# Renumbering the FFN units of a fused HGRN2 and FFN kernel, and pacing its weight loads by landings

## Chip, cores and metric

One core of one Trainium2 chip. The metric is the device time of one execution in microseconds; a kernel is run three to six times beside the kernel before on the same chip. Some executions fall in a slower state; medians below are over all runs.

## The reference

```python
f = 1 / (1 + exp(-f_logit))                       # (4, 8, 768, 48) each of q, k, v, f_logit
for t in range(768):
    state = f[t][:, None] * state + outer(k[t], v[t])
    y[t]  = q[t] @ state
x = y.transpose(0, 2, 1, 3).reshape(3072, 384)
h = maximum(x @ w_in, 0)                          # w_in (384, 2048)
out = (h * h) @ w_out                             # w_out (2048, 384)
```

The kernel cuts the sequence into 24 chunks of 128 tokens. The 2,048 FFN units may stand in any order, as long as the columns of w_in and the rows of w_out are renumbered alike.

## The kernel before

A small planner simulates the engines with fixed durations and settles the order of instructions on each. The kernel is then emitted in that order, and the framework puts in the semaphore waits. The weights come in eight pieces, cast by DMAs that GpSimd issues; the loads of f, k, q and v, 192 KB each in 192-byte runs, come through SyncE's queue.

```python
LOADS = [0, 1, 2, "i0", 3, "i1", "i2", "i3", "o0", "o1", 4, "o2", "o3"] + list(range(5, NCH))
...
w_in = const.tile([C, KS, d_ff], BF16)            # 128 x 3 x 2048
w_out = const.tile([C, FS, d_model], BF16)        # 128 x 16 x 384
wi_view = moe_w_in.rearrange("(ks p) f -> p ks f", p=C)
wo_view = moe_w_out.rearrange("(fs p) f -> p fs f", p=C)

def load_w(kind, s, behind):                      # piece s of w_in or w_out, set off by v of a chunk
    def fn():
        if kind == "i":
            nc.gpsimd.dma_start(w_in[:, :, s * FW:(s + 1) * FW], wi_view[:, :, s * FW:(s + 1) * FW])
        else:
            nc.gpsimd.dma_start(w_out[:, s * FQ:(s + 1) * FQ, :], wo_view[:, s * FQ:(s + 1) * FQ, :])
    plan.add(f"cw{kind}{s}", "POOL", 1.0, fn, after=[f"vc.{behind}"], rank=-1, data=(2.4, 0))
...                                               # attention: cut
for x in range(m):                                # first FFN product, hp
    for ks in range(KS):
        nc.tensor.matmul(hp[:, x, :], w_in[:, ks, (f + x) * C:(f + x + 1) * C], xT[:, ks, lo:lo + W], ...)
...                                               # relu and square, then the second product, op
nc.tensor.matmul(st["o", i], hT[:, fs, tt * C:(tt + 1) * C], w_out[:, fs, :], ...)
```

GpSimd also casts v (vz) and computes the state update (sz), which needs tm from VectorE, which needs ds from TensorE. Every engine runs its own instructions in order.

## Time and profile before

| | before |
|---|---|
| median, lowest, highest of 3 runs | 192.5, 192.18, 196.64 us |
| span of the profiled run | 192.4 us |
| useful TensorE work, all | 161.6 us |
| useful TensorE work by 50 us, by 60 us | 23.7, 33.7 us |

"Useful" is the sum over matmuls of columns / 2.4 + 2.5 ns, idle fillers left out; the prediction explains it. The sums come out only if each matmul counts for at least 26 ns. The narrow ones, of 1 and 48 columns, do follow one another at 25 to 26 ns in the trace; without this floor the figures are 159.1, 23.1 us. The profiled run itself took 194.19 us. In timelines the columns are start, duration, engine, line, operation, and in brackets the idle time just before and what ended it. The lines that carry the reading are in the prediction.

### The profile page before, as it was taken

What the parts mean: (1) busy time and instruction counts of PE and PEld (TensorE: products, weight loads), DVE (VectorE), ACT (ScalarE), POOL (GpSimd) and SP (SyncE); (2) the same over time, 40 slices, a digit from 0 to 9 for tenths busy, and PEclk for the clock granted to TensorE, in tenths of its full rate; (3) what the DMA queues carried; (4) which work ended last, traced back from release to release, by engine and by line L of the source; (5) the groups of instructions that cost most, each with busy time, mean ns of one, the idle gap of its engine ahead of it and who ended that gap; (6) DMA issues with size and microseconds to landing.
All of it is one profiled execution on the core that took longest, in us unless ns stands there. A gap on an engine that the chain in (4) does not pass through costs nothing.

```text
span 192.4 us, 4720 instructions
## 1 busy us (share of the span) xinstructions
PE 177.5 (92%) x1810; PEld 119.9 (62%) x1810; DVE 126.6 (66%) x262; ACT 129.4 (67%) x275; POOL 45.0 (23%) x87
## 2 busy tenths in 40 slices
PE   6783999938999999999999999999999999999992
PEld 5562788924777867666666666666566566656561
DVE  5683647742688998997996787889668724244200
ACT  4451278811577968999999887988777766376410
POOL 5251941010403423504231331232231100000000
PEclk9998599985999999999999999999999999999999
DMA  6999999999999999198999899996989896311112
GB/s 120 191 151 199 172 193 184 187 165 197 188 160 200 163 174 197 24 193 167 177 180 173 157 201 191 169 187 128 186 157 171 266 303 233 97 41 41 46 43 79
DMA packets 123255, 31.05 MB, mean 161 GB/s; under 512 B 116576, under 2 KB 123232, under 8 KB 123232
## 3 DMA queue, kind: packets, MB, share of 16 engines
q1 hardware_dynamic: 119520, 27.60, 78.4%
q0 software_dynamic: 3712, 3.15, 10.4%
q8 instruction: 14, 0.23, 0.5%
q14 instruction: 9, 0.07, 0.1%
HBM read 25.17 MB, written 4.72 MB: 155 GB/s over the span
## 4 chain that ended last, share of the span: by engine, by line
PE 70%; DMA 10%; SPq 10%; ACT 3%; DVE 2%; issue 2%
PE op L491 33%; PE hp L446 25%; DMA io_q<-in_q_dram 10%; SPq L217 10%; PE at L344 3%; PE yp L367 3%; PE pc L288 1%; PE tr L320 1%; PE ds L407 1%; PE xp L381 1%; ACT hr L453 1%; ACT ob L501 1%; DVE hr L455 1%; PE pc L291 1%; ACT hT L460 0%
## 5 line engine op out<-in xcount | busy, mean ns | idle before, releaser
L446 PE MATMUL hp<-xT,w_in 128*128 128x384 bf16 (+2 forms) x528 | 79.9, 285 | 0.3 <-DVE xT L386 0.2
L491 PE MATMUL op<-w_out,hT 128*128 128x384 bf16 x384 | 79.6, 332 | 0.6 <-ACT ob L501 0.6
L453 ACT ACTIVATE hr<-hp 128x384 bf16<-128x384 f32 (+1 forms) x102 | 52.0, 512 | 24.5 <-PE hp L446 21.6
L446 PEld LDWEIGHTS <-w_in 128*128 128x128 bf16 x528 | 42.4, 99 | 18.0 <-issue 0.8
L462 DVE TENSOR_TENSOR hT<-hr 128x384 bf16<-128x384 bf16 (+1 forms) x87 | 33.4, 385 | 30.4 <-ACT hr L453 28.9
L491 PEld LDWEIGHTS <-hT 128*128 128x128 bf16 x384 | 36.0, 99 | 23.8 <-issue 2.9
L424 POOL TENSOR_TENSOR sz<-tm,en 48x192 bf16<-48x192 f32 x40 | 22.2, 555 | 68.8 <-DVE tm L415 26.5
L351 DVE TENSOR_TENSOR am<-at,ut 128x512 bf16<-128x512 f32 x48 | 31.6, 683 | 2.7 <-PE at L344 2.5
L282 POOL CAST vz<-io_v 128x384 bf16<-128x384 f32 x24 | 13.8, 583 | 38.1 <-DMA io_v<-in_v_dram 37.5
L501 ACT COPY ob<-op 128x384 f32<-128x384 f32 x21 | 10.0, 476 | 17.2 <-PE op L491 17.1
L460 ACT ACTIVATE hT<-hr 128x384 bf16<-128x384 bf16 (+1 forms) x33 | 17.8, 540 | 1.7 <-DVE hr L455 0.8
L277 ACT ACTIVATE e<-io_f 128x384 f32<-128x384 f32 x24 | 12.5, 522 | 9.1 <-DMA io_f<-in_f_logit_dram 9.1
L308 DVE TENSOR_TENSOR az<-io_k,ep 128x384 bf16<-128x384 f32 x24 | 14.3, 594 | 3.5 <-ACT ep L298 3.3
L312 DVE TENSOR_TENSOR az<-io_q,en 128x384 bf16<-128x384 f32 x24 | 15.2, 631 | 1.5 <-DMA io_q<-in_q_dram 1.4
L298 ACT ACTIVATE ep<-pc 128x384 f32<-128x384 f32 x24 | 11.7, 488 | 5.0 <-PE pc L291 2.4
L415 DVE TENSOR_TENSOR tm<-ds,sz 128x384 f32<-128x384 f32 x16 | 8.8, 550 | 8.4 <-PE ds L407 7.9
L278 ACT ACTIVATE pz<-e 128x384 bf16<-128x384 f32 x24 | 12.6, 523 | 0.8
L304 ACT ACTIVATE en<-pc 128x388 f32<-128x388 f32 (+1 forms) x24 | 11.8, 492 | 0.0
L522 PE MATMUL idle<-zero 128*128 128x128 bf16 x108 | 10.7, 247 | 1.0 <-DVE zero L247 1.0
L455 DVE TENSOR_SCALAR hr<-hp 128x384 bf16<-128x384 f32 (+1 forms) x18 | 10.3, 574 | 1.7 <-PE hp L446 1.7
L344 PE MATMUL at<-ts 64*128 64x128 bf16 x192 | 10.0, 226 | 0.8 <-DVE ts L328 0.8
L320 PE MATMUL tr<-ident,az 128*128 128x128 bf16 x88 | 7.7, 224 | 3.0 <-DVE az L312 2.4
(40 smaller groups left out, 135.2 us busy)
## 6 DMA issues: line engine op xcount, KB each, us to landing
io_f<-in_f_logit_dram SPq DMA_DIRECT2D x24, 192.0 KB, 4.2
io_k<-in_k_dram SPq DMA_DIRECT2D x24, 192.0 KB, 4.3
io_q<-in_q_dram SPq DMA_DIRECT2D x24, 192.0 KB, 4.3
io_v<-in_v_dram SPq DMA_DIRECT2D x24, 192.0 KB, 4.2
out_dram<-ob SPq DMA_DIRECT2D x24, 192.0 KB, 2.6
w_in<-in_moe_w_in_dram POOLq DMA_DIRECT2D x4, 384.0 KB, 7.7
w_out<-in_moe_w_out_dram POOLq DMA_DIRECT2D x4, 384.0 KB, 14.7
ts<-az SPq DMA_TRANSPOSE x13, 3.5
```

The costliest lines, as they stand in the source:

```text
L217: nc.sync.dma_start(t, srcs[n][b].rearrange("h s d -> s h d")[c * C:(c + 1) * C])
L282: nc.gpsimd.tensor_copy(vz[i % 4], st["v", i])
L308: nc.vector.tensor_mul(az[i % 4][:, H:, :D], st["k", i], st["ep", i])
L312: nc.vector.tensor_mul(az[i % 4][:, :H, :D], st["q", i], st["en", i][:, :HD].rearrange("p (h d) -> p h d", d=D))
L344: nc.tensor.matmul(ps[x][:, pr, :], ts[r, NP + pr, :], ts[r, pr, :], skip_group_check=True)
L351: nc.vector.tensor_mul(t, st["at", i][x], ut4)
L424: nc.gpsimd.tensor_mul(nx[r, :, D * x:D * (x + 1)], st["tm", i][r, :, D * x:D * (x + 1)], st["en", i][r, HD:HD + NP].unsqueeze(2).to_broad ...
L446: nc.tensor.matmul(hp[:, x, :], w_in[:, ks, (f + x) * C:(f + x + 1) * C], xT[:, ks, lo:lo + W], start=(ks == 0), stop=(ks == KS - 1), skip ...
L453: nc.scalar.activation(hr[:, :m, :], st["hp", c0, f][:, :m, :], AFT.Relu)
L460: nc.scalar.activation(st["hT", g][:, f:f + m, lo:lo + W], hr[:, :m, :], AFT.Square)
L462: nc.vector.tensor_mul(st["hT", g][:, f:f + m, lo:lo + W], hr[:, :m, :], hr[:, :m, :])
L491: nc.tensor.matmul(st["o", i], hT[:, fs, tt * C:(tt + 1) * C], w_out[:, fs, :], start=(fs == 0), stop=(fs == FS - 1))
```

## The change

The intent is twofold. With four consecutive w_out rows in one partition, a DMA writes runs of 3,072 bytes instead of 768. And each weight piece is now set off when a named load has landed (a one-element copy, `touch`, makes GpSimd wait for it), so that pieces and loads share the DMA engines more evenly; the planner models the two rings for this, and puts the casts of v ahead of the pieces (`rank=-2`).

```diff
+    SHARE = {"POOL": 0.7, "SP": 0.3}             # planner: how two busy rings share (rest of it cut)
-    LOADS = [0, 1, 2, "i0", 3, "i1", "i2", "i3", "o0", "o1", 4, "o2", "o3"] + list(range(5, NCH))
+    PACE = [4, 8, 10, 13, 13, 17, 18, 18]        # piece n goes behind this many loads
-    wo_view = moe_w_out.rearrange("(fs p) f -> p fs f", p=C)
+    wo_view = moe_w_out.rearrange("(s p x) f -> p s x f", p=C, x=FQ)
+            if pace and x != "v":
+                nc.gpsimd.tensor_copy(touch[:1, :1], st[x, c][:1, 0, :1])
-                nc.gpsimd.dma_start(w_out[:, s * FQ:(s + 1) * FQ, :], wo_view[:, s * FQ:(s + 1) * FQ, :])
+                nc.gpsimd.dma_start(w_out[:, s * FQ:(s + 1) * FQ, :], wo_view[:, s])
...
-                        nc.tensor.matmul(hp[:, x, :], w_in[:, ks, (f + x) * C:(f + x + 1) * C], xT[...],
+                        nc.tensor.matmul(hp[:, x, :], units(ks, f + x), xT[...],
...
+    def units(ks, f):                            # every fourth column of a piece
+        s, x = divmod(f, FQ)
+        return w_in[:, ks, s * FW:(s + 1) * FW].rearrange("k (p x) -> k x p", x=FQ)[:, x]
```

More of the change, by code (lines that the diff above doesn't have):

```diff
@@ L77, in can, with done @@
             return True
+        def done(n, eng, end, fin):
+            s = left[n]
+            self.fin[n] = fin
+            heapq.heappush(events, fin)
+            for x in s.give:
+                heapq.heappush(gives, (fin, tuple(x.split(":"))))
+            for u in users.get(n, ()):
+                waiting[u] -= 1
+                at = ready_at.setdefault(u, {e: 0.0 for e in left[u].ways})
+                for e in at:
+                    at[e] = max(at[e], end if e == eng and s.land == self.LAT and not s.data else fin)
+                    heapq.heappush(events, at[e])
+                if waiting[u] == 0:
+                    release(u, at)
@@ new lines, in order, with heads, speed, next_move @@
+        rings = {"SP": [], "POOL": []}
+        clock = [0.0]
+        full = {}
+        self.fin = {}
+        def heads(t):
+            return {e: r[0] for e, r in rings.items() if r and r[0][2] <= t + 1e-9}
+        def speed(e, act):
+            return 1.0 if len(act) == 1 else self.SHARE[e]
+        def next_move():
+            t, act = clock[0], heads(clock[0])
+            ends = [t + x[3] / speed(e, act) for e, x in act.items()]
+            ends += [r[0][2] for r in rings.values() if r and r[0][2] > t + 1e-9]
+            return min(ends) if ends else None
@@ new lines, in advance @@
+        def advance(to):
+            while True:
+                nxt = next_move()
+                upto = to if nxt is None else min(nxt, to)
+                act = heads(clock[0])
+                for e, x in act.items():
+                    x[3] -= (upto - clock[0]) * speed(e, act)
+                clock[0] = max(clock[0], upto)
+                for e, x in act.items():
+                    if x[3] <= 1e-6:
+                        rings[e].pop(0)
+                        done(x[0], x[1], clock[0], clock[0] + self.RECEIPT)
+                if nxt is None or nxt > to:
+                    break
+            for e in list(full):
+                n, size, dur = full[e]
+                if sum(x[4] for x in rings[e]) + size <= self.RING:
+                    del full[e]
+                    post(n, e, max(to, ran[n][0] + dur))
@@ L79, in order, with post @@
+        def post(n, eng, end):
+            us, size = left[n].data
+            rings[eng].append([n, eng, end + self.FIRST, us, size])
+            avail[eng] = end
+            ran[n] = (ran[n][0], end, eng)
+            heapq.heappush(events, end)
         t, busy, count = 0.0, 0.0, 0
-        moved_to, queue = 0.0, []
         while count < len(left):
+            advance(t)
             while gives and gives[0][0] <= t + 1e-9:
@@ L111, in order @@
                     end = t + dur
-                    if s.data:
-                        us, size = s.data
-                        while size and sum(z for e, z in queue if e > end) + size > self.RING:
-                            end = min(e for e, z in queue if e > end)
-                        moved_to = max(moved_to, end + self.FIRST) + us
-                        queue.append((moved_to, size))
+                    ran[n] = (t, end, eng)
                     avail[eng] = end
-                    ran[n] = (t, end, eng)
                     if fill and eng == "PE":
@@ L126, in order @@
                     count += 1
-                    heapq.heappush(events, end)
-                    fin = moved_to + self.RECEIPT if s.data else end + s.land
-                    heapq.heappush(events, fin)
-                    for x in s.give:
-                        heapq.heappush(gives, (fin, tuple(x.split(":"))))
-                    for u in users.get(n, ()):
-                        waiting[u] -= 1
-                        at = ready_at.setdefault(u, {e: 0.0 for e in left[u].ways})
-                        for e in at:
-                            at[e] = max(at[e], end if e == eng and s.land == self.LAT else fin)
-                            heapq.heappush(events, at[e])
-                        if waiting[u] == 0:
-                            release(u, at)
+                    if s.data:
+                        us, size = s.data
+                        if sum(x[4] for x in rings[eng]) + size > self.RING:
+                            avail[eng] = float("inf")
+                            full[eng] = (n, size, dur)
+                        else:
+                            post(n, eng, end)
+                    else:
+                        heapq.heappush(events, end)
+                        done(n, eng, end, end + s.land)
                     moved = True
@@ L144, in order @@
             if count < len(left):
-                assert events, ("stuck", [n for e in ready.values() for n in e][:20])
-                t = events[0]
+                nxt = next_move()
+                assert events or nxt is not None, ("stuck", [n for e in ready.values() for n in e][:20])
+                t = min([x for x in (events[0] if events else None, nxt) if x is not None])
         self.ran = ran
@@ L179 @@
     HTB = 3
-    LOADS = [0, 1, 2, "i0", 3, "i1", "i2", "i3", "o0", "o1", 4, "o2", "o3"] + list(range(5, NCH))
-    LOADS = [x if isinstance(x, int) else (x[0], int(x[1])) for x in LOADS]
+    PACE = [4, 8, 10, 13, 13, 17, 18, 18]
     FILL = 40.0
@@ L226, with load_w @@
     wi_view = moe_w_in.rearrange("(ks p) f -> p ks f", p=C)
-    wo_view = moe_w_out.rearrange("(fs p) f -> p fs f", p=C)
-    def load_w(kind, s, behind):
+    wo_view = moe_w_out.rearrange("(s p x) f -> p s x f", p=C, x=FQ)
+    def load_w(kind, s, pace):
+        c, x = divmod(pace - 1, 4)
+        x = "fkqv"[x]
         def fn():
+            if pace and x != "v":
+                nc.gpsimd.tensor_copy(touch[:1, :1], st[x, c][:1, 0, :1])
             if kind == "i":
@@ L234, in fn @@
             else:
-                nc.gpsimd.dma_start(w_out[:, s * FQ:(s + 1) * FQ, :], wo_view[:, s * FQ:(s + 1) * FQ, :])
-        plan.add(f"cw{kind}{s}", "POOL", 1.0, fn, after=[f"vc.{behind}"], rank=-1, data=(2.4, 0))
-    for x in LOADS:
-        if isinstance(x, int):
-            load(x)
-            chunk = x
-        else:
-            load_w(x[0], x[1], max(chunk - 1, 0))
+                nc.gpsimd.dma_start(w_out[:, s * FQ:(s + 1) * FQ, :], wo_view[:, s])
+        after = [] if not pace else [f"vc.{c}"] if x == "v" else [f"{x}{c}"]
+        plan.add(f"cw{kind}{s}", "POOL", 0.8, fn, after=after, rank=-1, data=(2.6 if kind == "i" else 2.3, 0))
+    touch = const.tile([C, 1], F32)
+    for c in range(NCH):
+        load(c)
+    for n, pace in enumerate(PACE):
+        load_w("io"[n // NW], n % NW, pace)
     zero = const.tile([C, C], BF16)
@@ L282, in vc @@
             nc.gpsimd.tensor_copy(vz[i % 4], st["v", i])
-        plan.add(f"vc.{i}", "POOL", 0.52, vc, after=[f"v{i}"], take=["vz"], give=[f"io_v:v{i}"])
+        plan.add(f"vc.{i}", "POOL", 0.52, vc, after=[f"v{i}"], take=["vz"], give=[f"io_v:v{i}"], rank=-2)
         def p1():
@@ L445, in pe @@
                     for ks in range(KS):
-                        nc.tensor.matmul(hp[:, x, :], w_in[:, ks, (f + x) * C:(f + x + 1) * C], xT[:, ks, lo:lo + W],
+                        nc.tensor.matmul(hp[:, x, :], units(ks, f + x), xT[:, ks, lo:lo + W],
                                          start=(ks == 0), stop=(ks == KS - 1), skip_group_check=True)
```

## The prediction

> **What bounds the kernel now.** I began with the page: the busy line and the slices.
>
> ```profile
> PE 177.5 (92%) x1810; PEld 119.9 (62%) x1810; DVE 126.6 (66%) x262; ACT 129.4 (67%) x275; POOL 45.0 (23%) x87
> ...
> PE   6783999938999999999999999999999999999992
> ...
> PEclk9998599985999999999999999999999999999999
> DMA  6999999999999999198999899996989896311112
> ```
>
> The reader is to see two stages. TensorE is full from slice 11 (about 50 us) to the end. Before that it has holes, and two slices at half clock, while the DMA engines are full from the first slice on. Busy time counts overlapping matmuls, so I made a better ledger: each matmul is worth columns / 2.4 + 2.5 ns. The trace confirms it: the last 48 matmuls of 384 columns take 7.81 us, 163 ns each. Summed over the trace, hp is 62.8 us, op 62.4 us and the attention matmuls 36.4 us: 161.6 us of useful work in a span of 192.4. The gaps between matmul starts, compared with these costs, give under 1 us of loss from 50 to 188 us, some 4 us in the last evictions and stores, and **26.3 us lost before 50 us** (23.7 useful). The change can only win there.
>
> Next I read the early stage in the timelines of TensorE, then of the load queue:
>
> ```profile
> 19.02 0.48 PE L407 MATMUL ds<-vz,az 128*128 128x96 bf16 x4 [3.15 <-POOL vz L282]
> ...
> 21.02 2.77 PE L446 MATMUL hp<-xT,w_in 128*128 128x256 bf16 x12
> ...
> 39.06 0.39 PE L320 MATMUL tr<-ident,az 128*128 128x128 bf16 x4
> 41.83 0.61 PE L320 MATMUL tr<-ident,az 128*128 128x128 bf16 x4 [2.38 <-DVE az L312]
> 43.22 0.61 PE L344 MATMUL at<-ts 64*128 64x128 bf16 x8 [0.79 <-DVE ts L328]
> 43.76 3.38 PE L491 MATMUL op<-w_out,hT 128*128 128x384 bf16 x10
> 47.71 1.01 PE L491 MATMUL op<-w_out,hT 128*128 128x384 bf16 x3 [0.57 <-ACT ob L501]
> ```
> ```profile
> 21.19 5.19 SPq L217 DMA_DIRECT2D io_q<-in_q_dram  x1
> 26.42 5.08 SPq L217 DMA_DIRECT2D io_v<-in_v_dram  x1
> 31.54 5.54 SPq L217 DMA_DIRECT2D io_f<-in_f_logit_dram  x1
> 37.12 4.46 SPq L217 DMA_DIRECT2D io_k<-in_k_dram  x1
> 41.62 0.85 SPq L217 DMA_DIRECT2D io_q<-in_q_dram  x1
> ```
>
> The first FFN matmul starts at 21.0 us. TensorE waits 3.15 us for v of chunk 2 and again from 39.4 us for q of chunk 4; afterwards the clock is halved (the next 10 op matmuls take some 3.3 us instead of 1.63). The load queue, normally one issue a us, needs 5 us each while weights are moving. GpSimd's timeline gives the cause:
>
> ```profile
> 11.93 0.93 POOL L233 DMA_DIRECT2D w_in<-in_moe_w_in_dram  x1
> ...
> 18.92 2.34 POOL L233 DMA_DIRECT2D w_in<-in_moe_w_in_dram  x3
> 21.26 1.52 POOL L235 DMA_DIRECT2D w_out<-in_moe_w_out_dram  x2
> ```
>
> One piece goes at 11.9 us, then seven pieces at once from 18.9 us, and for 20 us nearly only weights move.
>
> **What the Trainium skill says.** (1) "TensorE: Matmul & The Clock Gate", Back-to-back issue gap: N / 2.4 + 2.5 ns warm. The trace agrees at 163 ns. (2) "DMA: Bandwidth & Descriptors", Queues, rings and completion order: each engine goes round the rings packet by packet. The trace's packet records agree: between 32 and 38 us each 2 us hold about 380 packets of w_out (768 B) and 390 of the loads (192 B), one for one. So a ring with large packets starves one with small packets. (3) Same page, Anatomy of one DMA: most of the fixed cost is the write receipt. Here v of chunk 1 has its last packet at 10.4 us and its consumer starts at 11.40: 1.0 us. (4) "TensorE: Matmul & The Clock Gate", Weight-path perf modes: the fast weight load takes packed or strided columns, steps up to 1,024 elements. The kernel before has no strided weight load, so no run shows it yet.
>
> **The change, part by part.** *Arithmetic:* unchanged. Both instruction orders hold the same matmuls of every shape (hp 48 of 256 columns, 192 of 128, 288 of 384; op 384; attention alike); only idle fillers go from 108 to 122, and they lie in gaps. So the 161.6 us stay.
>
> *Strided weight load:* hp takes every fourth column of w_in. If the load (now 95 to 99 ns, 62% busy) stays below 163 ns, it is hidden behind 384-column matmuls. Only the 192 matmuls of 128 columns, which now follow each other at 60 ns (36 between 36.39 and 38.57 us), are exposed: 20 ns more on each would cost 3.8 us, part of it in gaps. I expect 0.
>
> *Longer runs:* w_out goes from 2,048 packets to 512. A piece moved beside loads takes 2.67 us now (landings at 32.0, 34.7, 37.4, 40.1 us). The two packet pairs, 84 ns for 768 B and 110 ns for 1,024 B, extrapolate to 246 to 318 ns for 3,072 B; eight a piece and engine make 2.0 to 2.5 us; I take 2.2, an estimate. Saved: 4 x 0.45 = 1.9 us of weight traffic. But one packet for one packet, the loads pass only 8 of their 64 packets an engine during a piece instead of 32: 96 packets x 16 ns = 1.5 us of loads are put off. Net about 0.4 us: **the longer runs alone are nearly neutral.**
>
> *Pacing:* the pieces go behind v0, v1, k2, f3, f3, f4, k4, k4 in place of v1 and v2, v3. I wrote a schedule of landings by hand from three numbers: a load alone every 1.03 us (from 2.95 us on), a w_in piece 2.64 us with 24 load packets passing, a w_out piece 2.2 us with 8; plus 1 us of receipt and 0.9 us of issue, and the order in GpSimd's queue, where state updates stand ahead of the triggers. Usable times in us, before -> estimated after: first w_in piece 18 -> 13; second 26 -> 18.5; third 28 -> 21; fourth 31 -> 31; last w_out piece 42.5 -> 40; v2 18.4 -> 22; q4 41.2 -> 38.5; v4 42.7 -> 41. The engines are full in both, so the last of these move only by 1 to 3 us; the first three move by 5 to 7.
>
> *TensorE on this schedule:* first hp at 17 us instead of 21.0. Then a hole of some 3 us until q2 (21.5 us), because the next matmuls in its order are the transposes of chunk 2. From 23 to 36 us work is at hand. Then a wait for q4 of about 2 us in place of 2.4 plus 0.8, with 24 hp matmuls of chunk 3 (1.45 us) still to do after it. At 41.5 us I count 20.7 useful us (hp 10.6, op 1.0, attention 9.1), so 20.8 lost; I add 2 us for half clock after the holes (before: 3.4). Lost 22.8 instead of 26.3: **3.5 us won** on paper, 189.0. For hand-made optimism (each wait that I did not see costs) I give back 0.8: 189.8 us.
>
> **Rivals.** *(A) Loads starved by big packets.* If q4 loses its race with the second w_out piece, it trickles at 8 packets a piece and arrives near 41 us, as before; TensorE then stands from 36 to 41.5 us and goes into half clock again. For it: one-for-one packets and 5 us issues above. Against: q4 needs only a few packets more by my schedule. Time: 192 to 193.
>
> *(B) The early start counts fully.* If the hole at 18 to 21 us is filled and the clock stays up before and after, the 3.4 us of half clock and the 0.6 us wait for the eviction vanish too: 26.3 - 7 gives 185.5 to 187.5. For it: the page shows PEclk 5 in two slices. Against: the order still puts chunk 4's transposes ahead of hp work that is ready.
>
> *(C) Hidden anyway.* TensorE is full after 50 us, but its order is new. If evictions or DMA transposes now stop it for 2 us later, the gain is eaten: 191 to 192. For: ScalarE and VectorE are 80 to 100% busy from 60 to 100 us. Against: the loss there is now under 1 us and the order is nearly the same from the first 384-column hp on.
>
> *(D) Strided weight loads slow.* 3 to 5 us more, 193 to 197.
>
> **Range and chances.** The centre is 189.8. A gives the upper edge, 193; B the lower, 186.5. Faster by over 2% means below 188.65: that needs most of B; I give 0.34. Slower by over 2% means above 196.35: only D together with A; 0.04. The rest, 0.62, within 2%.
>
> **What would show each step right or wrong.** Packets: 512 of 3,072 B, near 250 ns, and a w_out piece about 2.2 us after the other. Pacing: issues of loads no longer in a run of four at 5 us, but several stretches. First hp near 17 us; no long wait for q4; the half-clock windows before 50 us fewer or shorter. Useful work by 50 us: 27 instead of 23.7, and the gain in the end equal to that difference. Weight loads of w_in still 95 to 100 ns. After 50 us under 1 us of loss. The prediction is wrong if the wait for q4 or v4 has grown (A), if 128-column hp matmuls are spaced above 60 ns (D), or if holes open after 60 us (C).

## The result

The changed kernel takes **204.31 us** (median of 4 runs, 202.33 to 204.86; before 192.34 over its 4 runs). The ratio is 1.0623, 95% interval 1.0522 to 1.0724: slower by about 6%. Here and below a ratio is the mean time of one kernel's fast runs over that of the other's fast runs of the same rounds, so it is not quite the ratio of the medians quoted.

The page of the changed kernel, the same slices:

```profile
PE 179.2 (88%) x1824; PEld 127.7 (63%) x1824; DVE 125.7 (62%) x259; ACT 129.7 (64%) x278; POOL 44.0 (22%) x93
...
PE   6973382398989999999999999999999999999992
...
PEclk9999599579999999999999999999999999999999
DMA  6999999999999800009999999898877966821112
```

TensorE now has two deep holes, near 20 and 35 us, and the DMA engines stand idle for four slices (71 to 91 us), where before only one slice was nearly idle. By 60 us only 23.6 us of useful work are done, where the kernel before had 33.7: 10.1 us behind, and the two profiled runs differ by 10.5 us (204.65 and 194.19). So nearly all of the loss between these two runs arises before 60 us. (The profile before is of a slow run; between the means of fast runs, 203.95 and 191.98, the loss is 12.0 us.) TensorE's timeline shows where:

```profile
16.74 0.27 PE L505 MATMUL hp<-xT,w_in 128*128 128x256 bf16 x1 [0.17 <-DVE xT L445]
23.57 2.51 PE L505 MATMUL hp<-xT,w_in 128*128 128x256 bf16 x11 [6.56 <-DMA w_in<-in_moe_w_in_dram]
...
31.33 0.87 PE L505 MATMUL hp<-xT,w_in 128*128 128x256 bf16 x7
38.93 1.36 PE L505 MATMUL hp<-xT,w_in 128*128 128x128 bf16 x11 [6.73 <-DMA w_in<-in_moe_w_in_dram]
```

The first FFN matmul starts at 16.74 us, as forecast. The second, of the same piece, waits 6.56 us for w_in; after the group at 31.33 us TensorE stops again, for 6.73 us. For a while after each stop the granted clock was 0.50 (23 to 26 and 38 to 40 us). Yet the trace's packet records have the first piece landed at 13.4 us, the second at 17.0. What had just landed when TensorE went on was the *third* piece (23.1 us), and at the second stop the *fourth* (38.6 us). The matmuls that waited need neither. GpSimd's timeline:

```profile
17.14 0.81 POOL L292 DMA_DIRECT2D w_in<-in_moe_w_in_dram  x1
18.17 0.50 POOL L341 CAST vz<-io_v 128x384 bf16<-128x384 f32 x1 [0.22 <-DMA io_v<-in_v_dram]
30.33 1.07 POOL L483 TENSOR_TENSOR sz<-tm,en 48x192 bf16<-48x192 f32 x2 [11.66 <-DVE tm L474]
31.46 0.18 POOL L290 COPY touch<-io_f 1x1 f32<-1x1 f32 x1
32.45 0.80 POOL L292 DMA_DIRECT2D w_in<-in_moe_w_in_dram  x1 [0.81 <-PE hp L505]
```

The fourth piece is issued at 32.45 us. Its trigger, f of chunk 3, had its last packet at 18.5 us. It stood behind a state update that waited for TensorE, and then, last of all, **it waited itself for an FFN matmul** (0.81 us, in brackets). The first piece of w_out goes at 33.4 us; the other three follow behind the next state update, from 48 us, and the last lands at 57.3 us.

The built program confirms both. This is its listing of instructions with the semaphores that each waits for (not a profile; Ldweights is a weight load, and DMASW0 to 3 are the four w_in pieces); first the kernel before, then the changed one:

```
before:   L446 Ldweights w_in [waits DMASW0_49]          first
          L446 Ldweights w_in                            second
changed:  L505 Ldweights w_in [waits DMASW0_49]          first
          L505 Ldweights w_in [waits DMASW2_49,DMASW1_49]   second: false
          ...
          L292 DMACopy w_in<-in_moe_w_in_dram 128x3x512 [waits PE_49]   fourth piece: false
```

The likely reason: a piece covers three separate runs of 512 elements in the free dimension of w_in (128 x 3 x 2048). Measured from its first to its last element, piece 1 spans 512 to 5,120. The packed slice of 128 elements was told apart from that; the strided slice seems to be compared by its outer span. For the first matmul (row block 0, elements 0 to 512) this touches no other piece, and it waits for its own alone; for the second (row block 1, 2,048 to 2,560) it falls inside the span of all others. This fits the listing, but how the framework decides was inferred, not seen.

### The profile page after: what moved, and what is told of

Same layout as the page of the kernel before. It is cut to its first block, busy times and chain, and to the rows that moved or that the text cites. A ratio compares the mean times of both kernels' runs of the same rounds, so it can differ in the third digit from the quotient of the medians.

```text
span 202.9 us, 4744 instructions
## 1 busy us (share of the span) xinstructions
PE 179.2 (88%) x1824; PEld 127.7 (63%) x1824; DVE 125.7 (62%) x259; ACT 129.7 (64%) x278; POOL 44.0 (22%) x93
## 4 chain that ended last, share of the span: by engine, by line
PE 77%; DMA 8%; ACT 7%; DVE 4%; issue 2%; POOL 1%; ACTq 0%; POOLq 0%
PE hp L505 30%; PE op L556 30%; DMA w_in<-in_moe_w_in_dram 6%; PE at L403 3%; PE yp L426 3%; ACT hr L512 3%; PE tr L379 2%; PE pc L347 2%; PE xp L440 2%; ACT hT L519 2%; DVE ts L387 1%; DMA io_f<-in_f_logit_dram 1%; PE idle L587 1%; PE ds L466 1%; DVE am L410 1%
## 5 line engine op out<-in xcount | busy, mean ns | idle before, releaser
L505 PE MATMUL hp<-xT,w_in 128*128 128x384 bf16 (+2 forms) x528 | 82.4, 292 | 14.0 <-DMA w_in<-in_moe_w_in_dram 13.3
L512 ACT ACTIVATE hr<-hp 128x384 bf16<-128x384 f32 (+1 forms) x98 | 50.0, 511 | 43.5 <-PE hp L505 41.5
L556 PE MATMUL op<-w_out,hT 128*128 128x384 bf16 x384 | 77.5, 326 | 0.2
L505 PEld LDWEIGHTS <-w_in 128*128 128x128 bf16 x528 | 49.2, 117 | 29.5 <-issue 7.8
L521 DVE TENSOR_TENSOR hT<-hr 128x384 bf16<-128x384 bf16 (+1 forms) x80 | 30.6, 387 | 43.6 <-ACT hr L512 41.9
L519 ACT ACTIVATE hT<-hr 128x384 bf16<-128x384 bf16 (+1 forms) x40 | 21.8, 546 | 2.4 <-DVE hr L514 1.3
L566 ACT COPY ob<-op 128x384 f32<-128x384 f32 x22 | 10.5, 476 | 11.0 <-PE op L556 11.0
L514 DVE TENSOR_SCALAR hr<-hp 128x384 bf16<-128x384 f32 (+1 forms) x22 | 12.8, 580 | 3.2 <-PE hp L505 3.2
L587 PE MATMUL idle<-zero 128*128 128x128 bf16 x122 | 12.5, 255 | 1.0 <-DVE zero L306 1.0
L587 PEld LDWEIGHTS <-zero 128*128 128x128 bf16 x122 | 9.6, 116 | 1.3 <-DVE zero L306 1.0
L387 DVE COPY ts<-tr 128x1024 bf16<-128x1024 bf16 x11 | 7.6, 688 | 4.2 <-PE tr L379 4.1
```

Of the source, the lines that this page charges most:

```text
L505: nc.tensor.matmul(hp[:, x, :], units(ks, f + x), xT[:, ks, lo:lo + W], start=(ks == 0), stop=(ks == KS - 1), skip_group_check=True)
L512: nc.scalar.activation(hr[:, :m, :], st["hp", c0, f][:, :m, :], AFT.Relu)
L519: nc.scalar.activation(st["hT", g][:, f:f + m, lo:lo + W], hr[:, :m, :], AFT.Square)
L521: nc.vector.tensor_mul(st["hT", g][:, f:f + m, lo:lo + W], hr[:, :m, :], hr[:, :m, :])
L587: nc.tensor.matmul(idle, zero, zero)
```

## Experiments

Twelve runs were made, of eleven kernels. They are told in the order of the argument: 10 and 11 ran beside 5, before 6 to 9. By the 2% rule the record calls the comparison with the kernel before unclear in all of them but the last ("same"), so the argument rests on twins (the same instructions in the same order, with and without the false waits; each pair but that of experiment 1 ran on one chip) and on the traces. Theory **F** is that these false waits are the loss. Its rivals are **P**, the pacing itself (triggers behind state updates), and **S**, the strided weight load as such.

### 1. The changed kernel with w_in stored piece by piece

```diff
-    w_in = const.tile([C, KS, d_ff], BF16)
+    w_in = const.tile([C, NW, KS, FW], BF16)
-                nc.gpsimd.dma_start(w_in[:, :, s * FW:(s + 1) * FW], wi_view[...])
+                nc.gpsimd.dma_start(w_in[:, s], wi_view[...])
-        return w_in[:, ks, s * FW:(s + 1) * FW].rearrange("k (p x) -> k x p", x=FQ)[:, x]
+        return w_in[:, s, ks, :].rearrange("k (p x) -> k x p", x=FQ)[:, x]
```

The instructions of every engine and their order are those of the changed kernel; only addresses in SBUF and waits differ. The DMA packets are the same too: 1,536 of 1,024 bytes and 512 of 3,072.

> The changed kernel, with w_in kept piece by piece in its tile, so that the strided read of one piece no longer spans the others. Theory F (the strided read is taken for an access of all pieces, and these false waits are the whole loss): no wait of TensorE for w_in over 2 us, the fourth w_in piece is issued before 28 us instead of at 32.5 us, and the time is 187 to 193 us. Rival P (the pacing itself, triggers that stand behind state updates in GpSimd's queue, is at fault): the last piece of w_out is still issued after 40 us and the time is 198 us or more.

Measured: **189.23 us** (187.43 to 190.41; ratio to before 0.9788, 0.9675 to 0.9901; only two of its four runs count as fast). The listing has each piece waited for once, at its first use. TensorE's timeline of this kernel, at the two places that stopped before:

```profile
17.37 2.26 PE L505 MATMUL hp<-xT,w_in 128*128 128x256 bf16 x12 [0.17 <-DVE xT L445]
...
32.21 2.35 PE L505 MATMUL hp<-xT,w_in 128*128 128x256 bf16 x24 [0.66 <-DMA w_in<-in_moe_w_in_dram]
```

All twelve matmuls of the first piece run at once, and the only wait for w_in is 0.66 us. The fourth piece is issued at 25.4 us. Useful work by 60 us is 37.7 us, some 14 more than in the changed kernel, whose profiled run took 204.65 against 190.29 us here (a slow one of this kernel's runs): 14.4. The two kernels ran on different chips, but the kernel before is alike there: its fast runs have a mean of 191.98 us beside the changed kernel and 191.87 beside this one. F holds; P falls as the main cause, since the pacing is the same. S falls too: the strided loads are all still there, at the same 113 ns (median).

### 2. The pacing alone, units not renumbered

```diff
-    wo_view = moe_w_out.rearrange("(s p x) f -> p s x f", p=C, x=FQ)
+    wo_view = moe_w_out.rearrange("(s x p) f -> p s x f", p=C, x=FQ)
-        return w_in[:, ks, s * FW:(s + 1) * FW].rearrange("k (p x) -> k x p", x=FQ)[:, x]
+        return w_in[:, ks, f * C:(f + 1) * C]
```

> The new pacing and planner, but the units keep their old numbers: packed weight loads and w_out rows one at a time. Theory F: no false waits, so within 1.5 us of the piece-major kernel (187 to 193 us). Rival P: 198 us or more. Rival S (strided weight loads cost time): this is 3 us or more faster than the piece-major kernel.

Measured: **187.92 us** (187.57 to 189.38; ratio 0.9809, 0.9725 to 0.9892), within the spread of experiment 1. No false waits, no loss: the pacing is sound.

### 3 and 4. The renumbering alone, without and with w_in piece by piece

Both start from the kernel before and keep its pacing. Experiment 3 takes over `units` and the view of w_out alone; experiment 4 adds the layout of experiment 1.

```diff
-    wo_view = moe_w_out.rearrange("(fs p) f -> p fs f", p=C)
+    wo_view = moe_w_out.rearrange("(s p x) f -> p s x f", p=C, x=FQ)
-    nc.tensor.matmul(hp[:, x, :], w_in[:, ks, (f + x) * C:(f + x + 1) * C], ...
+    nc.tensor.matmul(hp[:, x, :], units(ks, f + x), ...
```

> The kernel before, with the renumbering only. Its second weight load now waits for all four w_in pieces. Theory F: the first FFN matmuls stop from 21 us to about 31 us (the fourth piece lands at 30.4 us), some of this is made up later, and the time is 195 to 201 us, though the pacing is the old one. Rival P: 191 to 194 us, since the pacing is unchanged.

> The kernel before with the renumbering and w_in kept piece by piece: longer runs and strided loads, old pacing, no false waits. Theory F with neutral long runs: 190.5 to 193.5 us, w_out pieces 2.2 us apart instead of 2.67. Rival S: 195 us or more.

Measured: **198.01 us** (ratio 1.0312, 1.0192 to 1.0432) and **194.75 us** (ratio 1.0141, 1.0063 to 1.0219). TensorE's timeline of experiment 3:

```profile
18.07 0.27 PE L446 MATMUL hp<-xT,w_in 128*128 128x256 bf16 x1
27.88 2.51 PE L446 MATMUL hp<-xT,w_in 128*128 128x256 bf16 x11 [9.54 <-DMA w_in<-in_moe_w_in_dram]
```

The second matmul waits 9.54 us, for the fourth piece (landed 27.5 us). All pieces are issued before the first FFN matmul here, so no DMA waits for TensorE, and of the 9.5 us only 3.3 us remain between the twins: at 30 us experiment 3 is 6.3 us of useful work behind experiment 4, at 60 us only 2.7, since experiment 4 in its turn waits for a load (below).

Experiment 4 missed its 190.5 to 193.5. The traces point to the long runs: by themselves they are not neutral under the old pacing. SyncE's and TensorE's timelines of experiment 4:

```profile
21.69 8.43 SPq L217 DMA_DIRECT2D io_k<-in_k_dram  x1
```
```profile
33.89 0.48 PE L407 MATMUL ds<-vz,az 128*128 128x96 bf16 x4 [4.61 <-POOL vz L282]
```

One load issue is held up for 8.43 us (5.5 at most before), and TensorE waits 4.61 us for v of chunk 3, which the kernel before had at 24 us. Between 28 and 30 us the packet records hold 125 packets of 3,072 bytes at 247 ns and 146 of 192 bytes, where the kernel before let some 390 of these pass in 2 us beside packets of 768: near one for one both times, so a longer weight packet lets proportionally fewer load packets past. This is the forecast's rival A, at the old pacing. No run has the long runs without the strided loads, so the 1.4% is not split by an experiment; but 36 matmuls of 128 columns take 2.35 us in both kernels, so the strided loads are hidden here too. Under the new pacing experiments 1 and 2 do not show it beyond their spread.

### 5. The fourth piece ahead of the state update

`PACE = [4, 8, 10, 10, 13, 17, 18, 18]` in the changed kernel, false waits kept.

> The changed kernel with its false waits, but the fourth w_in piece is set off by k2, like the third, so that in GpSimd's queue it stands ahead of the state update of chunk 2. It still has the false wait on TensorE's first FFN group (a DMA waits until the reads before it are done). Theory F with a loop (TensorE waits for a piece, the state update waits for TensorE, the next piece waits for the state update): the second wait for w_in shrinks or ends near 31 us instead of 38.9 us, and the time is 198 to 202 us, better than 204 but far from 189. Without the loop, only the false waits themselves counting: 203 to 206 us.

Measured: **206.72 us** (203.63 to 207.57; the two fast runs 203.63 and 205.89): a miss for the loop. It fits the other forecast, 203 to 206 us with the false waits alone. The second stop did end at 30.5 us, near the 31 that I expected, but the time did not follow. TensorE's timeline, then GpSimd's:

```profile
22.19 1.45 PE L505 MATMUL hp<-xT,w_in 128*128 128x256 bf16 x6 [5.67 <-DMA w_in<-in_moe_w_in_dram]
30.48 1.26 PE L505 MATMUL hp<-xT,w_in 128*128 128x256 bf16 x5 [6.84 <-DMA w_in<-in_moe_w_in_dram]
```
```profile
23.73 0.78 POOL L292 DMA_DIRECT2D w_in<-in_moe_w_in_dram  x1 [6.38 <-PE hp L505]
```

The fourth piece, though first in GpSimd's queue, waits 6.38 us for the first FFN group, and the next group then waits 6.84 us for that piece. TensorE and the DMA hold each other up in turn without any state update. So the role that I had given to the state updates was in doubt, and two pairs of twins were made.

### 6 and 7. Only one direction of the false wait

`PACE = [4, 8, 8, 8, 13, 17, 18, 18]` sets off pieces two to four together, before the first FFN matmul in the program. Experiment 6 has the changed kernel's layout, experiment 7 the piece-major one.

> The changed kernel with its strided reads over all of w_in, but pieces two to four of w_in all set off by v1, so that all four DMAs stand ahead of the first FFN matmul in the program and none has to wait for TensorE. What is left is one false wait of the first FFN group for the fourth piece (near 21 us). Theory F2 (the large loss comes from the false wait in the other direction, a piece held back until TensorE has read the earlier ones, in turn with the first): 191 to 196 us, 2 to 5 us above its piece-major twin. If the false waits of TensorE alone make the loss: 199 us or more.

> The twin of the run before it with w_in kept piece by piece: the same program order, no false waits. The healthy level for this pacing: 188 to 192 us.

Measured: **198.37 us** (ratio 1.0266) and **194.49 us** (ratio 1.0098). Both levels are some 2.5 us above the ranges that I wrote, but the difference, 3.9 us, is inside the 2 to 5. Experiment 6 has one wait of 6.96 us for w_in, and no DMA of w_in waits for TensorE:

```profile
24.08 2.51 PE L505 MATMUL hp<-xT,w_in 128*128 128x256 bf16 x11 [6.96 <-DMA w_in<-in_moe_w_in_dram]
```

So with TensorE waiting falsely only once, 3.3 us (experiments 3 and 4) or 3.9 us are lost, not 15.

### 8 and 9. The state update on VectorE

```diff
-                nc.gpsimd.tensor_mul(nx[r, ...
+                nc.vector.tensor_mul(nx[r, ...
-        plan.add(f"s2.{i}", "POOL", 1.0, s2, ...
+        plan.add(f"s2.{i}", "DVE", 0.6, s2, ...
```

> The changed kernel with its false waits, with the state update moved from GpSimd to VectorE, so that no piece is behind a state update in GpSimd's queue. If the state updates in GpSimd's queue are a needed part of the loss: 9 us or less above its piece-major twin, with w_out all landed before 47 us. If the false wait of the DMA for TensorE suffices: 12 to 16 us above the twin.

> The twin of the run before it with w_in kept piece by piece. VectorE gets some 20 us of state updates at a load of 67%; pieces come as soon as their trigger has landed: 186 to 191 us.

Measured: **206.82 us** (ratio 1.0707) with the changed kernel's layout and **193.37 us** (ratio 1.0021) with the piece-major one: 13.4 us apart, inside the 12 to 16 (the second level is above the 186 to 191 that I wrote). They are apart though nothing but casts of v stands ahead of a trigger in GpSimd's queue now, and w_out has landed by 43.3 us. GpSimd's timeline of the first, then TensorE's:

```profile
29.43 0.78 POOL L292 DMA_DIRECT2D w_in<-in_moe_w_in_dram  x1 [7.63 <-PE hp L505]
```
```profile
20.73 2.34 PE L505 MATMUL hp<-xT,w_in 128*128 128x256 bf16 x11 [3.38 <-DMA w_in<-in_moe_w_in_dram]
...
35.48 1.36 PE L505 MATMUL hp<-xT,w_in 128*128 128x128 bf16 x11 [6.24 <-DMA w_in<-in_moe_w_in_dram]
```

The fourth piece waits 7.63 us for TensorE instead of for the state update, and TensorE stops twice as before. The state updates are one way in which the fourth piece is held back, but not a needed one; the false wait of the DMA for TensorE suffices.

### 10 and 11. Triggers ahead of the state updates in the healthy kernels

`PACE = [4, 8, 10, 12, 12, 16, 17, 17]`, with packed columns (from experiment 2) and piece-major with the renumbering (from experiment 1).

> The pacing-alone kernel (no renumbering), with the pieces set off a little earlier (v0, v1, k2, v2, v2, v3, f4, f4), which puts three of the triggers ahead of a state update in GpSimd's queue. If the state updates that stand ahead of the triggers still cost in the healthy kernel: the fourth w_in piece is issued near 19 us instead of 23.5 us and the time is 185 to 187 us. If the full DMA engines are all that counts: within 1 us of the pacing-alone kernel, 187 to 190 us.

> The same earlier triggers in the piece-major kernel with the renumbering. If the long w_out packets starve the loads when they come early (as in the kernel before with renumbering and piece-major w_in, 194.75 us): 190 us or more, and slower than its packed twin by 2 us or more. If pacing protects the loads: within 1 us of the packed twin.

Measured: **190.77 us** (ratio 0.9919) and **190.98 us** (ratio 0.9957). The fourth piece was issued at 19.9 us instead of 23.5, and yet the time did not fall: 0.9919 (0.9828 to 1.001) against 0.9809, on other chips. Both runs lie above the 187 to 190 us that I wrote for this case. The medians of the twins agree within 0.3 us, so the long runs cost nothing that these runs resolve under such pacing. Setting the pieces off earlier gained nothing that these runs resolve.

### 12. The pacing alone once more

The kernel of experiment 2, unchanged, five rounds on another chip.

> The pacing-alone kernel again on another chip with five rounds, to see how far the best version beats the kernel before: a ratio of 0.975 to 0.988. If its lead came from slow runs of the kernel before, the ratio is within 0.5% of 1.

Measured: **189.29 us** (188.24 to 190.93, six fast runs) against 192.05; ratio 0.9907, 0.9848 to 0.9965. That is outside the 0.975 to 0.988 that I wrote, and nearer to 1 than on the first chip. The pacing without false waits beats the kernel before, and the changed one by far, but by 1 to 2%, not clearly by 2%.

## Why the prediction was wrong

- **The step that failed** is the one headed "Strided weight load", which ends "I expect 0". It priced only the duration of the load. The load did get longer, 113 ns (median) instead of 98, and this did stay hidden: 24 matmuls of 128 columns start at 51.10 us and the next group at 52.44, 56 ns each. But the strided form changed which DMAs the framework makes the load wait for, and that was worth 15.1 us between the medians of the changed kernel and of experiment 1 (204.31 and 189.23; not the same chip). The kernel's waits were taken to be those before. The listing of the built program would have shown two more semaphores on the second weight load and one on the fourth piece, and I did not look at it.
- **None of the rivals named it.** A and D came nearest: D (strided loads slow) pointed the right way, but its 193 to 197 us ends 7 us short, and the runs refute its reason.
- **Pacing.** The schedule of landings failed with the waits: fourth piece usable at 31 us, in fact near 39; last w_out piece at 40, in fact near 58 (57.3 landed, and the receipt). In experiment 1, where the false waits are gone, the fourth piece is used at 32.2 us and the last w_out piece lands at 42.3: the hand schedule was right to 1 to 3 us for the kernel that I thought I had.
- **First FFN matmul** near 17 us: right, 16.74, but for one matmul only.
- **TensorE's sum**, 3.5 us won and 189.8 us: wrong for the changed kernel, and close to what experiment 1 gives without the false waits (189.23 us; 27.8 us of useful work by 50 us, forecast 27). This is partly luck: the two waits for q in the sum, of 3 and 2 us, are not in its timeline, where after the first FFN matmul TensorE never waits longer than 0.73 us for anything; some half clock and many short waits stand in their place.
- **Longer runs.** 512 packets near 250 ns and pieces 2.2 us apart: measured 247 to 248 ns (10th to 90th percentile), and 2.0 us (53.3, 55.3 and 57.3 us). "The longer runs alone are nearly neutral" fell: 194.75 us, 1.4% over before, in experiment 4. The term for loads put off, 1.5 us, left out that the load put off was the one TensorE needed next.
- **Readings of the profile.** GpSimd set off five pieces from 18.9 us and two more from 24.6, not seven at once. The lower figure for a long packet, 246 ns, does not follow from the two pairs given (they give 318); the packet alone took 247 ns, and in experiment 4 a pair took 256 (16 engines x 2 us / 125). The receipt of 1.0 us is that of a load in SyncE's queue, while the section cited is about the path through GpSimd; there the changed kernel's third piece had its last packet at 23.1 us and its semaphore at 23.4.
- **After 60 us** TensorE is full, as expected. The four idle slices of the DMA engines cost nothing there.

Open: how the framework compares regions; and whether, under the new pacing, the long runs gain or lose the half percent that these runs cannot resolve.

## What to carry to other kernels

When an access changes its form (packed to strided, one region to a view), look at the waits in the built program before pricing durations: a false dependency costs nothing in busy time and can cost far more than the instruction. A wait for a DMA that ends when a *different* piece lands, and a load that waits for a matmul that reads something else, are its marks in a profile. Store pieces that arrive separately so that each is one closed range, and be the more careful about this the more the pieces are spread in time: with all pieces early the same false wait cost 3 to 4 us, with pieces spread out and held back in turn 13 to 15 us (medians of twins).

## What the Trainium skill lacked or had wrong

- "TensorE: Matmul & The Clock Gate", Weight-path perf modes, lists strided columns beside packed ones for the fast weight load and gives no price for the step. Here a step of four bf16 elements took 113 ns a load (median) against 98 ns packed, hidden behind matmuls down to 128 columns at 56 ns each.
- "DMA: Bandwidth & Descriptors", Queues, rings and completion order: rings are served packet by packet. The runs agree near enough (125 long and 146 short packets in 2 us), but the page draws no consequence for a ring of short packets: in experiment 4 one load issue was held up for 8.43 us, from 21.7 to 26 us beside 1,024-byte packets and then beside 3,072-byte ones, against 5.5 us at most in the kernel before.
- No page that I read says that a strided read of a tile can bring waits for DMAs into other parts of it. Here it cost 15.1 us of 204.3 (medians, experiment 1).
